# Resident tokens, a reordered program, PSUM banks given out by the list scheduler and a table of priorities in a gated convolution-and-MLP kernel

## The chip, the cores and the metric

The kernel runs on one core of a Trainium2 chip. The time is the device time of one execution in microseconds (us). Every kernel was also timed beside the kernel before on the same chip. The profile is one execution taken by the hardware profiler; its times count from its own first instruction, so a span is some 2 us shorter than the device time. Engines are named as in the profile: PE is TensorE (PEld its weight loads), DVE is VectorE, ACT is ScalarE, POOL is GpSimd, SP is SyncE and SPq its instruction queue, which only issues DMA transfers here.

## The reference

There are 2048 tokens of 640 values. A sigmoid gate, computed from each token, mixes two branches. Branch A is a four-tap convolution of k, times v, then a long convolution over the sequence, times q. Branch B is an MLP of four layers with two layer-norms and shifts by one or two tokens.

```
x  = A_q;  g = sigmoid((x * gate_w).sum(-1))
# branch A
k_shift[t] = sum over j of k[t - j] * shift_k[:, j]        # 4 taps, per channel
kv = k_shift * v
a  = q * (irfft(rfft(pad(kv)) * rfft(pad(ssm_k)))[:2048] + kv * ssm_D)
# branch B
h  = gelu(layernorm(x) @ w1)                               # 640 -> 640
hs = (the four quarters of h shifted by +1, -1, +2, -2 tokens) @ w2
x1 = x + hs
b  = x1 + gelu(layernorm(x1) @ w3) @ w4                    # 640 -> 1536 -> 640
out = g * a + (1 - g) * b
```

The kernels replace the FFT by folded Fourier transforms in blocks, done as matrix products: forward transforms of kv and of the filter, products of the spectra on VectorE (eight "units", one for each of four frequency groups and two channel halves) and inverse transforms.

## The kernel before

Every operation is recorded with the buffers it reads and writes, an engine and an estimated duration. A list scheduler then simulates the five engines and fixes the order of each engine's instructions when the kernel is built; on the chip the engines run these orders strictly in sequence and wait for one another by semaphores.

```
def schedule(self, bw=250.0, tbw=90.0, dlat=1900.0, lat=90.0, backlog=2500.0):
    ...
        for e in ENGS:                                   # pe, act, dve, pool, sp
            ...
            f = free[e]
            for i in cand[e]:                            # whose predecessors are placed
                st = max(f, ready[i])
                ...
                key = (st, -(ops[i].rank + ops[i].bias), i)     # rank: longest way to the end
                if pick is None or key < pick:
                    pick = key
            if best is None or pick < best:
                best = pick
    ...                                                  # the winner is next in its engine's order
```

The biases are all zero in this kernel. The second MLP layer reloads each token tile, adds it in a matrix product, and sends every tile through four engines and a DMA transpose:

```
def mm2(t):
    P.dma(sp, xr[t % 3], A_q[0, 128 * t:128 * (t + 1), :])
    b = mlp_bank()                            # four PSUM banks in a ring for the MLP
    ...
    act(x1[t % 3]..., pr, ACTF.Copy, accum=st[1, 0][:, t:t + 1])
    act(xn2[t % 3], x1[t % 3], ACTF.Square, accum=st[1, 1][:, t:t + 1])
    P.dma(sp, x1s[128 * t:128 * (t + 1), :], x1[t % 3])          # "scratch store"
def ln2(t0, t1):
    ln_math(1, t0, t1)                        # 6 small GpSimd operations
    ... ln_apply: one VectorE operation, then a DMA transpose issued by SyncE
```

The last fifth of the first layer is evicted straight to its four shifted places, 32 partitions at a time:

```
for g in range(4):
    act(hT[32 * g:32 * (g + 1), 4, c0:c0 + 512], ps(b)[32 * g:32 * (g + 1), :], ACTF.Gelu_apprx_tanh)
```

Of the kernel before, what the change touches and what calls it, by code (L numbers as in the profile page):

```python
# [10 lines left out]
BANK = 2048  # L11


class Op:
    __slots__ = ("idx", "eng", "fns", "ins", "outs", "dur", "bias", "nbytes", "preds", "succs", "rank",
                 "tp", "ordinal", "waits", "inc", "value", "dsem", "dval", "snap", "snapd", "start", "end", "order")

    def __init__(self, idx, eng, fns, ins, outs, dur, bias, nbytes):
        self.idx = idx
        self.eng = eng  # L20
        self.fns = fns
        self.ins = ins
        self.outs = outs
        self.dur = dur
        self.bias = bias
        self.nbytes = nbytes
        self.preds = {}
        self.succs = []
        self.inc = False
        self.dsem = None  # L30
        self.tp = False

# [42 lines left out]
def regions(ap):  # L75

    t = ap.tensor
# [3 lines left out]
    if not name.startswith(("arena", "PS")):  # L81
        lo = ap.offset + sum(min(0, s * (n - 1)) for s, n in dims)
        hi = ap.offset + sum(max(0, s * (n - 1)) for s, n in dims) + 1
        return [(name, 0, lo * esz, hi * esz)]
# [12 lines left out]
    psum = name.startswith("PS")  # L97
    out = set()
    for lo, hi in runs:
        b0, b1 = (f0 + lo) * esz, (f0 + hi) * esz  # L100
        if psum:
            b0, b1 = b0 // BANK * BANK, -(-b1 // BANK) * BANK
        for q in range(p0 // 32, (p0 + pcnt - 1) // 32 + 1):
            out.add(("PS" if psum else "SB", q, b0, b1))
# [3 lines left out]
class Prog:  # L108
    def __init__(self, nc):
# [3 lines left out]
        self.bias = 0.0  # L113

    def _record(self, op):
        idx = op.idx
        op.bias += self.bias
# [6 lines left out]
        for ap in op.ins:  # L124
            for reg in regions(ap):
                (ws if reg[0] == "PS" else rs).append(reg)
        for ap in op.outs:
            ws.extend(regions(ap))
        for m, q, lo, hi in rs:
# [17 lines left out]
    def dma(self, queue, out, in_, bias=0.0, transpose=False, slow=False):  # L147
# [9 lines left out]
        issue = 1300.0 if transpose else (700.0 if queue == "pool" else 400.0)  # L157
# [5 lines left out]
    def schedule(self, bw=250.0, tbw=90.0, dlat=1900.0, lat=90.0, backlog=2500.0):  # L163
        ops = self.ops
        for o in ops:
            for p in o.preds:
                ops[p].succs.append(o.idx)
        for o in reversed(ops):
            tail = 0.0
            for s in o.succs:  # L170
                tail = max(tail, ops[s].rank)
            full = o.dur + (o.nbytes / bw + dlat if o.nbytes else lat)
            o.rank = max(tail + full, 0.0)
        left = [len(o.preds) for o in ops]
        ready = [0.0] * len(ops)
        cand = {e: [] for e in ENGS}
        free = {e: 0.0 for e in ENGS}
        dfree = tfree = 0.0
        for o in ops:
            if left[o.idx] == 0:  # L180
                cand[o.eng].append(o.idx)
        order = []
        while True:
            best = None
            for e in ENGS:
                if not cand[e]:
                    continue
                f = free[e]
                pick = None
                for i in cand[e]:  # L190
                    st = max(f, ready[i])
                    if ops[i].nbytes and not ops[i].tp:
                        st = max(st, dfree - backlog)
                    key = (st, -(ops[i].rank + ops[i].bias), i)
                    if pick is None or key < pick:
                        pick = key
                if best is None or pick < best:
                    best = pick
            if best is None:
                break  # L200
            st, _, i = best
            o = ops[i]
            cand[o.eng].remove(i)
            o.start = st
# [4 lines left out]
            elif o.nbytes:  # L209
                t0 = max(st + 0.5 * o.dur, dfree)  # L210
                dfree = t0 + o.nbytes / bw
                o.end = max(dfree, st + o.dur) + dlat
            else:
                o.end = st + o.dur
            o.order = len(order)
            order.append(o)
            for s in o.succs:
                left[s] -= 1
                d = lat
                if ops[s].eng == o.eng and not o.nbytes:  # L220
                    d = 60.0 if ops[s].preds[i] and o.eng != "pe" else 0.0
# [3 lines left out]
        assert len(order) == len(ops)  # L225
# [131 lines left out]
def bass_gated_mix__ssm_conv_h3__mixer_s_mlp__prompt_kernel(  # L357
# [33 lines left out]
    def ps(b, n=1):  # L391
        return PSt[:, 512 * b:512 * (b + n)]

# [5 lines left out]
    oWB = alloc(15360)  # L399
# [6 lines left out]
    oXR = alloc(3 * 640)  # L406
    oX1 = alloc(3 * 640)
    oXN = alloc(3 * 640)
    oX1R = alloc(3 * 640)
# [3 lines left out]
    XF = V(oXF, 20480).rearrange("p (b j r d) -> p b j r d", b=4, j=4, r=2)  # L413
# [8 lines left out]
    w3 = V(oWB, 7680).rearrange("p (c f) -> p c f", c=5)  # L422
    w4 = V(oWB + 7680, 7680).rearrange("p (c f) -> p c f", c=12)
    keo = [V(oWB + 2560 * i, 2560).rearrange("p (e s d) -> p e s d", e=2, s=2) for i in range(2)]
    vin = [V(oWB + 5120 + 1280 * i, 1280).rearrange("p (s d) -> p s d", s=2) for i in range(2)]
    kin = [V(oWB + 7680 + 3200 * i, 3200).rearrange("p (i d) -> p i d", i=5) for i in range(2)]
    kv_hi = V(oWB + 14080, 1280).rearrange("p (s d) -> p s d", s=2)
    kv_lo = V(oPT + 3840, 1280).rearrange("p (s d) -> p s d", s=2)
    kv_rev = V(oX1R, 1280).rearrange("p (s d) -> p s d", s=2)
    kpr = V(oUT, 5120).rearrange("p (s j d) -> p s j d", s=2, j=4)  # L430
    kst = [V(oXF + 2048 * i, 2048).rearrange("p (b n) -> p b n", b=4) for i in range(2)]
    heo_c = [V(oXF + 4096 + 2048 * i, 2048) for i in range(2)]
    heo_t = [V(oXF + 8192 + 2048 * i, 2048) for i in range(2)]
    xT = [V(oXT + 2560 * i, 2560).rearrange("p (c s) -> p c s", c=5) for i in range(3)]
    SHK = V(oYX, 2560).rearrange("p (j d) -> p j d", j=4)
    xin = [V(oPT + 640 * i, 640) for i in range(3)]
    xn1 = [V(oPT + 1920 + 640 * i, 640) for i in range(3)]
# [3 lines left out]
    xr = [V(oXR + 640 * i, 640) for i in range(3)]  # L441
# [36 lines left out]
    def is_ps(ap):  # L478
        return ap.tensor.name.startswith("PS")

    def dve_ns(o, i, mode):
        n = n_of(o)
        if is_ps(o) or any(is_ps(a) for a in i):
# [3 lines left out]
    def tt(o, a, b, op, eng="dve"):  # L487
        P.op(eng, lambda e: e.tensor_tensor(o, a, b, op), [a, b], [o],  # L488
             dve_ns(o, [a, b], 2) if eng == "dve" else 250)

    def ts(o, a, s1, s2, op0, op1=None, eng="dve"):
        aps = [s for s in (s1, s2) if not isinstance(s, (int, float, type(None)))]
        P.op(eng, lambda e: e.tensor_scalar(o, a, s1, s2, op0=op0, **({} if op1 is None else {"op1": op1})),  # L493
             [a] + aps, [o], dve_ns(o, [a], 3) + 60 if eng == "dve" else 250)

    def act(o, a, f, scale=1.0, bias=0.0, accum=None):
        aps = [s for s in (scale, bias) if not isinstance(s, (int, float))]
        P.op("act", lambda e: e.activation(o, a, f, bias=bias, scale=scale, **({"accum_out": accum} if accum is not None else {})),  # L498
# [3 lines left out]
    def mm(o, pairs, split=None):  # L502

        fns = []
        for i, (l, r) in enumerate(pairs):
            fns.append(lambda e, l=l, r=r, i=i: e.matmul(o, l, r, start=(i == 0), stop=(i == len(pairs) - 1)))  # L506
        P.op("pe", fns, [a for p in pairs for a in p], [o], len(pairs) * max(60, n_of(o) / 2.4) + 5)

    sp = "sp"


    P.op("dve", lambda e: e.memset(neghalf, -0.5), [], [neghalf], 70)
# [6 lines left out]
    P.op("dve", lambda e: e.memset(hT[96:128, 4, S:S + 2], 0.0), [], [hT[96:128, 4, S:S + 2]], 70)  # L519
    act(tjunk[:, 1:2], ones[:, 0:1], ACTF.Gelu_apprx_tanh)  # L520
    P.dma("pool", shk_sb.rearrange("p (c j) -> p c j", c=5), A_shift_k.rearrange("(c p) j -> p c j", p=128))
    P.dma("pool", V(oId, 256).bitcast(U16), cI.ap())
    P.dma("pool", Esel.bitcast(U16), cE.ap())
    P.dma("pool", Dcol.rearrange("p (c o) -> p c o", o=1), A_ssm_D.rearrange("(c p o) -> p c o", p=128, o=1), slow=True)
    P.dma("pool", gwT.rearrange("p (c o) -> p c o", o=1), gate_w.rearrange("(c p o) -> p c o", p=128, o=1), slow=True)
    P.dma("pool", V(oR, 2048).bitcast(U16), cR.ap())
    P.dma("pool", w1, B_w1.rearrange("(c p) f -> p c f", p=128))
    for c in range(DC):
        P.dma("pool", w1x[:, c, :].rearrange("p (g f) -> p g f", g=4),
              B_w1[c * 128:(c + 1) * 128, :].rearrange("p (g f) -> p g f", g=4)[:, :, 128:160])  # L530
    for j in range(4):
        P.dma("pool", w2[:, j, :], B_w2[160 * j:160 * j + 128, :])
    for g in range(4):
        P.dma("pool", w2[32 * g:32 * (g + 1), 4, :], B_w2[160 * g + 128:160 * g + 160, :])


    psb = ps(0).bitcast(BF16)
    P.op("pe", [lambda e, c=c: e.transpose(psb[0:4, 128 * c:128 * (c + 1)], shk_sb[:, 4 * c:4 * c + 4], ident)  # L538
                for c in range(DC)], [shk_sb, ident], [psb[0:4, 0:640]], 400)
    act(rows4, psb[0:4, 0:640], ACTF.Copy)  # L540
    for j in range(4):
        pr = ps(2 * (j % 2), 2).rearrange("p (b n) -> p b n", b=2)[:, :, 0:320]
# [3 lines left out]
    mm(ps(0)[:, 0:1], [(ones, gwT[:, c:c + 1]) for c in range(DC)])  # L546
    act(gsum[:, 0:1], ps(0)[:, 0:1], ACTF.Copy)


    cb = [0]  # L550

    def conv_bank(n=1):
        if n == 2:
            b = 4 + 2 * (-(-cb[0] // 2) % 2)
            cb[0] = b - 4 + 2
        else:
            b = 4 + cb[0] % 4
            cb[0] += 1
        return b

    def h_load(c):
        k = kst[c % 2]
        P.dma(sp, k.rearrange("p b n -> p (b n)"), A_ssm_k[128 * c:128 * (c + 1), :])

    def h_chunk(c):
        k, ec, et = kst[c % 2], heo_c[c % 2], heo_t[c % 2]
# [7 lines left out]
        for y in range(4):  # L574
            eo = (0, 1, 1, 0)[y]
            for m in range(2):
                b = conv_bank()
                mm(ps(b), [(Rt[:, y, kk, 128 * m:128 * (m + 1)], ev[:, eo, kk, :]) for kk in range(2)])
                j, r = 2 * (y // 2) + m, y % 2
                src = ps(b).rearrange("p (b c) -> p b c", b=4)  # L580
                lo = 128 * c
                while lo < 128 * (c + 1):
                    hh = lo // 320
# [367 lines left out]
```

## Time and profile before

The median of three runs is 307.29 us (305.7 to 308.86).

| stretch (us) | what runs | limit |
|---|---|---|
| 0 to 91 | layer-norm 1, first layer, filter and k·v work | VectorE |
| 103 to 178.8 | second layer, 16 tiles through four engines and a DMA | latency of the tiles |
| 178.8 to 303.5 | third and fourth layer, inverse transforms | TensorE |

The first part of the page gives each engine's busy time, share and instruction count; the second shows the busy tenths in 40 slices of the span.

```profile
PE 249.3 (81%) x1526; PEld 144.0 (47%) x1526; DVE 229.0 (74%) x352; ACT 151.5 (49%) x289; POOL 87.8 (29%) x156
PE   0401949876797998747899599999999999999994
DVE  4489997989983934948879999999999991121343
```

The table of stretches gives from:to, length, then busy time and instruction count of PE, PEld, DVE, ACT and POOL, the granted clock, the DMA share and GB/s.

```profile
0.00:91.00 91.00, 52.78 (x286) 23.76 (x287) 76.21 (x118) 47.54 (x89) 28.81 (x48) 0.94 0.92 237
103.00:178.80 75.80, 61.60 (x364) 36.30 (x362) 57.54 (x84) 45.87 (x101) 54.41 (x99) 0.93 0.63 172
178.80:303.50 124.70, 124.61 (x816) 79.28 (x816) 87.39 (x142) 48.20 (x83) 1.78 (x5) 1.00 0.21 56
```

The chain of waits (start, length, what) ends in one piece of TensorE work. Below it stands the line for the scratch stores from the view of one tile: durations, then the first and last start.

```profile
171.47 5.74 DMA arena<-arena
178.80 124.63 PE PSall L506 x816
L156 SPq DMA_DIRECT2D x_scratch<-arena x16: 319/452/581, 107.5 to 175.7; - x16
```

So TensorE has nothing but work from 178.8 us on, and the question for any change is how much sooner that state can begin. The 16 tiles of the second layer stand alone from 107.5 to 175.7 us, at 4.5 us a tile.

### The profile page before, as it was taken

Reading aid. Unit: us, or ns where it says so; the run is one execution under the profiler, and the core shown is the slowest. Engines: PE = TensorE matmul, PEld = TensorE weight load, DVE = VectorE, ACT = ScalarE, POOL = GpSimd, SP = SyncE. Lnnn points to the kernel's source line nnn. Section 1 sums busy time; section 2 is a strip of 40 time slices with the busy share of each in tenths; the row PEclk is TensorE's granted clock in tenths of the full one; section 3 lists DMA queues with packets and bytes.
Section 4 is the critical chain, followed back from the end, with each engine's and each line's share of the span. In section 5 each row is a group of like instructions: output and inputs, shape, how many; then the busy total and the mean of one; then the engine's idle time right before and its main releaser. Section 6 shows DMA issues by size and latency. Waiting matters only on the chain.

```text
span 307.5 us, 4162 instructions
## 1 busy us (share of the span) xinstructions
PE 249.3 (81%) x1526; PEld 144.0 (47%) x1526; DVE 229.0 (74%) x352; ACT 151.5 (49%) x289; POOL 87.8 (29%) x156
## 2 busy tenths in 40 slices
PE   0401949876797998747899599999999999999994
PEld 0101314432353575424456357456645664777773
DVE  4489997989983934948879999999999991121343
ACT  1400577975588799732844321622462155333342
POOL 6265602021032256866968840000000000000000
PEclk9999997996999999887999799999999999999999
DMA  7978999978934047996633630004101311023342
GB/s 238 308 244 155 340 170 270 384 216 227 196 79 115 6 124 212 250 331 161 184 78 93 182 106 21 23 0 107 45 0 35 96 43 45 24 83 87 107 132 84
DMA packets 54708, 43.04 MB, mean 140 GB/s; under 512 B 34204, under 2 KB 50592, under 8 KB 54560
## 3 DMA queue, kind: packets, MB, share of 16 engines
q1 hardware_dynamic: 52848, 35.40, 44.8%
q0 software_dynamic: 1840, 7.39, 7.8%
q8 instruction: 12, 0.20, 0.3%
q14 instruction: 8, 0.07, 0.1%
HBM read 29.66 MB, written 5.24 MB: 114 GB/s over the span
## 4 chain that ended last, share of the span: by engine, by line
PE 52%; DVE 21%; DMA 11%; POOL 8%; ACT 4%; issue 3%; SPq 0%; ACTq 0%; POOLq 0%
PE PSall L506 51%; DVE arena L488 16%; DMA arena<-arena 8%; ACT arena L498 4%; POOL arena L652 3%; DVE arena L645 2%; POOL arena L488 2%; DMA arena<-in_A_shift_k_dram 2%; POOL arena L493 2%; DMA arena<-in_A_ssm_k_dram 2%; DVE arena L493 1%; POOL arena L661 1%; POOL arena L156 1%; DVE arena L646 1%; SPq L153 0%
## 5 line engine op out<-in xcount | busy, mean ns | idle before, releaser
L506 PE MATMUL PSall<-arena 128*128 128x320 bf16 (+3 forms) x1521 | 248.6, 323 | 46.2 <-ACT arena L498 14.2
L488 DVE TENSOR_TENSOR arena<-arena 128x640 bf16<-128x640 bf16 (+8 forms) x253 | 199.1, 836 | 51.0 <-ACT arena L498 43.4
L506 PEld LDWEIGHTS PSall<-arena 128*128 128x128 bf16 (+1 forms) x1521 | 143.5, 100 | 151.1 <-issue 32.5
L498 ACT ACTIVATE arena<-PSall 128x512 bf16<-128x512 f32 (+4 forms) x190 | 109.0, 613 | 85.6 <-PE PSall L506 68.5
L498 ACT ACTIVATE arena<-PSall,arena 128x320 bf16<-128x320 f32 (+1 forms) x48 | 29.5, 616 | 56.0 <-PE PSall L506 52.9
L493 POOL TENSOR_SCALAR arena<-arena 128x1 f32<-128x1 f32 (+2 forms) x44 | 23.0, 524 | 74.9 <-DVE arena L646 55.7
L493 DVE TENSOR_SCALAR arena<-arena 128x640 bf16<-128x640 bf16 (+2 forms) x36 | 15.5, 450 | 20.6 <-POOL arena L488 20.3
L488 POOL TENSOR_TENSOR arena<-arena 128x1 f32<-128x1 f32 (+2 forms) x60 | 24.4, 411 | 12.6 <-DVE arena L493 8.9
L498 ACT ACTIVATE arena<-arena 128x640 bf16<-128x640 bf16 (+2 forms) x18 | 12.2, 679 | 10.2 <-DMA arena<-arena 10.0
L645 DVE BATCH_NORM_STATS2 arena<-arena 128x6 f32<-128x320 bf16 x32 | 13.8, 473 | 3.0 <-DMA arena<-in_A_q_dram 3.0
L661 POOL TENSOR_TENSOR arena<-arena 128x1 f32<-128x1 f32 x16 | 12.9, 804 | 1.1
L156 POOL DMA_DIRECT2D arena<-in_B_w_dram x16 | 11.2, 703 | 2.6 <-PE PSall L506 2.6
L652 POOL TENSOR_TENSOR arena<-arena 128x2 f32<-128x2 f32 (+1 forms) x9 | 11.7, 1301 | 0.7
L538 PE MATMUL PSall<-arena 128*4 128x128 bf16 x5 | 0.7, 302 | 8.0 <-DMA arena<-in_A_shift_k_dram 8.0
L538 PEld LDWEIGHTS PSall<-arena 128*4 128x4 bf16 x5 | 0.4, 109 | 8.0 <-DMA arena<-in_A_shift_k_dram 8.0
L498 ACT ACTIVATION_READ_ACCUMULATOR arena<-PSall 128x1 f32 x16 | 3.2, 201 | 0.0
L646 DVE BATCH_NORM_AGGREGATE arena<-arena 128x2 f32<-128x12 f32 x16 | 3.1, 200 | 0.1
L498 ACT ACTIVATION_READ_ACCUMULATOR arena<-arena 128x1 f32 x16 | 3.1, 195 | 0.0
L498 ACT ACT_TABLE_LOAD x1 | 1.3, 1283 | 0.7 <-PEq L936 0.7
L770 DVE MEMSET arena<- 1x640 uint32 x2 | 1.2, 592 | 0.3 <-DVE arena L493 0.2
L156 POOL DMA_DIRECT2D arena<-in_A_ssm_D_dram x1 | 1.0, 999 | 0.0
L156 POOL DMA_DIRECT2D arena<-cI x1 | 0.8, 754 | 0.8 <-POOLq L936 0.8
(19 smaller groups left out, 6.1 us busy)
## 6 DMA issues: line engine op xcount, KB each, us to landing
arena<-in_A_q_dram SPq DMA_DIRECT2D x48, 160.0 KB, 3.3
arena<-in_A_k_dram SPq DMA_DIRECT2D x7, 800.0 KB, 5.7
arena<-in_B_w_dram POOLq DMA_DIRECT2D x2, 1920.0 KB, 10.1
arena<-in_A_ssm_k_dram SPq DMA_DIRECT2D x5, 512.0 KB, 5.0
arena<-in_A_v_dram SPq DMA_DIRECT2D x8, 320.0 KB, 4.4
x_scratch<-arena SPq DMA_DIRECT2D x16, 160.0 KB, 2.9
arena<-x_scratch SPq DMA_DIRECT2D x16, 160.0 KB, 2.3
out_dram<-arena SPq DMA_DIRECT2D x16, 160.0 KB, 2.3
```

Of the source, the lines that this page charges most:

```text
L156: fn = lambda e: e.dma_start(out, in_, **kw)
L488: P.op(eng, lambda e: e.tensor_tensor(o, a, b, op), [a, b], [o], dve_ns(o, [a, b], 2) if eng == "dve" else 250)
L493: P.op(eng, lambda e: e.tensor_scalar(o, a, s1, s2, op0=op0, **({} if op1 is None else {"op1": op1})), [a] + aps, [o], dve_ns(o, [a], 3) + ...
L498: P.op("act", lambda e: e.activation(o, a, f, bias=bias, scale=scale, **({"accum_out": accum} if accum is not None else {})), [a] + aps, [ ...
L506: fns.append(lambda e, l=l, r=r, i=i: e.matmul(o, l, r, start=(i == 0), stop=(i == len(pairs) - 1)))
L538: P.op("pe", [lambda e, c=c: e.transpose(psb[0:4, 128 * c:128 * (c + 1)], shk_sb[:, 4 * c:4 * c + 4], ident) for c in range(DC)], [shk_sb, ...
L645: P.op("dve", lambda e, o=o, i=i: e.bn_stats(o, i), [i], [o], 420)
L646: P.op("dve", lambda e: e.bn_aggr(bna[:, t, :], bns[k]), [bns[k]], [bna[:, t, :]], 130)
L652: P.op("pool", lambda g: g.tensor_tensor(r, e, neghalf[:, t0:t1], ALU.pow), [e, neghalf[:, t0:t1]], [r], 600)
L661: P.op("pool", lambda e: e.tensor_tensor(s[5], s[3], neghalf[:, t0:t1], ALU.pow), [s[3], neghalf[:, t0:t1]], [s[5]], 600)
L770: P.op("dve", lambda e: e.memset(H[0:1, 1], 0.0), [], [H[0:1, 1]], 400)
```

## The change

Its intent is to run the second layer's slow tile chain beside the k·v work and to take load off the early stage. It has six parts: the tokens stay in SBUF for the second layer; layer-norm 1 and the first layer come first in the program; the k·v work is split into two channel halves; PSUM banks are no longer fixed rings but given out by the scheduler; some transposes go from DMA to TensorE; and each group of operations gets a bias from a table of 389 numbers. The diff, cut to its core:

```diff
+    BIASES = {'combine-0-1|dve': 1782800.0,
+     'combine-0-2|dve': 287000.0,
...                                                 (389 entries, ns, from -2.7e6 to 2.9e6)
+    P.biases.update(BIASES)
     def schedule(self, quota, ...):                # PSUM: a bank is chosen when a tile's first
+                    if live[t.cls] >= quota[t.cls] or t.turn != turn[t.cls]:
+                        continue                   # operation is placed
-    def kv_half(b, hi, dst):
+    def kv_half(g, b, hi, dst):                    # 320 channels of k and v: runs of 640 bytes
+    keo, vin, kin, kv_hi in oW4                    # k·v staging shares w4's space
-        P.dma(sp, xr[t % 3], A_q[0, 128 * t:128 * (t + 1), :])
-            pairs.append((ident, xr[t % 3][:, hs]))
+            pairs.append((ident, xs[t // 4][:, t % 4, hs]))     # tokens are resident
-                for g in range(4):
-                    act(hT[32 * g:32 * (g + 1), 4, c0:c0 + 512], ps(b)[32 * g:..., :], Gelu)
+                act(hx[sc % 2], pr, ACTF.Gelu_apprx_tanh)       # one Gelu of 128 partitions
+                for g in range(4):                              # and four SBUF copies
+                    P.dma(sp, hT[32 * g:32 * (g + 1), 4, c0:c0 + 512], hx[sc % 2][32 * g:..., :])
+            if t >= PET:                                        # PET = 4: the first four tiles
+                ln_apply(...)                                   # are transposed on TensorE
+    for sc in range(4):                             # new program order
+        x_load(sc); ln1(...); mm1(sc)
+    gate; h_load and h_chunk; mm2 and ln2 of 12 tiles; w3_load; mm3(0); the other 4 tiles;
+    then kv_block, x_fwd and combine of both halves; w4_load; mm4(0..3); ...
```

The new layer-norm 2 also needs four GpSimd operations instead of six. The diff changes more than the six parts: the scheduler's own costs are new (a plain issue on SyncE costs 0.47 us instead of 0.40, a 128x640 transpose 1.46 instead of 1.30, a small GpSimd operation 0.45 instead of 0.25), loads of constants and of w1 go from GpSimd's queue to ScalarE's or SyncE's, and the q loads of the output stage go from SyncE's queue to GpSimd's.

## The prediction

> **What bounds the kernel now.** Three stages.
>
> - 0 to 91 us: VectorE. The stretches table gives it 7 to 10 us busy of every 10 from 10 us on: layer-norm 1, filter folding and the k·v preparation are interleaved. TensorE gets work only as VectorE delivers it.
> - 103 to 178 us: a latency chain. The 16 tiles of the second MLP layer pass through TensorE, ScalarE, GpSimd, VectorE and a DMA transpose, with three buffers. Their scratch stores (queue timeline) are issued from 107.5 to 175.7 us, 4.5 us a tile; VectorE is 5 to 10 us busy of 10 (it waits 43.4 us for ScalarE in all).
> - 178.8 to 303.5 us: TensorE. The chain of waits is one piece of 124.6 us with 816 matmuls; the stretches show 10.0 of 10 busy.
>
> TensorE is busy 249.3 us of 307.5. At the pace of the stretch 280 to 290 us (76 matmuls of 320 columns, 0.132 us each) its 1008 x 320 and 420 x 512 columns are, estimated, 222 us of work, 97 us of it before 178.8 us: about 80 us are lost there.
>
> **What the change does.**
>
> - Order: layer-norm 1 and the first MLP layer come first, so the 4.5 us-per-tile chain runs beside the k·v work, not after it. This is the main gain.
> - PSUM: eight shared banks placed by the scheduler, not two fixed rings (TensorE waited 14.2 us for ScalarE).
> - Tokens resident: 16 reloads of 160 KB and their 3.3 us landings go. Four DMA transposes (4.4 us to landing) become 20 TensorE transposes with ScalarE evictions.
> - ScalarE: sixteen 32-partition Gelus (589 ns) become four full ones (601 ns) plus 16 small DMAs, 7 us less. GpSimd: 4 instead of 6 operations per layer-norm-2 tile (414 to 804 ns each).
> - VectorE, estimated from measured shapes: k·v halves 8 x 5.94 = 47.5 us become 16 x 3.27 = 52.4; with folding and combining +7 us, on 229.
> - k and v are read in 640-byte runs. The Trainium skill ("DMA: Bandwidth & Descriptors", Specifications) wants 512 B for line rate, so I expect little loss; the trace cannot confirm it.
>
> **How much is critical.** A new gate: w4 takes the space of the k·v staging, so it loads (10.1 us) only after the last k·v block. VectorE's work until then is layer-norm 1 24 + filter 13 + k·v 60 + layer-norm-2 applies 7 = 104 us; with start-up and idle 115. w4 is there near 125 us. TensorE then still has mm4 55, mm3 of three chunks 38, inverse transforms 34 = 127 us, plus some 6 left over and a 4 us end: 262 us. VectorE's path (115 + combine 10 + eight units 103 + last inverse 17 + 4) ends near 249, so TensorE still finishes last.
>
> **Prediction: 262 us, range 249 to 281.** Faster by over 2%: 0.95; within 2%: 0.035; slower: 0.015.
>
> **What would show it.** Scratch stores start before 60 us and end near 115. The last k·v multiplication is near 110 us. The saturated TensorE piece that ends the chain starts near 130. TensorE busy falls by up to 15 us, VectorE rises to about 235, ScalarE falls to about 143.
>
> **What would make it wrong.** The hand-fed priorities fit a model, not the chip: in-order queues may stall behind one late transfer. The DMA traffic of the first 180 us (about 36 MB) must pass in some 125; if transposes and 640-byte runs limit it, everything shifts by 10 to 20 us. If VectorE ends last, the units set the end.

## The result, and the profile after

The changed kernel takes 284.4 us in the median (283.07 to 284.78, four runs) where the kernel before takes 308.08 beside it. The ratio is 0.925 (0.918 to 0.932). All ratios here are the mean time of one kernel's fast runs over that of the other's fast runs of the same rounds, so they are not quite the ratio of the medians. A control of the same kernel among the later runs gave 283.95 us and 0.922. The prediction of 262 us, and its range up to 281, were too optimistic.

The same lines of the page after the change:

```profile
PE 242.9 (86%) x1531; PEld 146.5 (52%) x1546; DVE 232.5 (82%) x399; ACT 142.5 (50%) x257; POOL 76.6 (27%) x124
PE   0078879939999959969999999979999999999994
DVE  3769797759889389866799999999999999999242
```

The busy times are nearly those predicted (VectorE "about 235", ScalarE "about 143"). What moved is the idle time. The stretches below end where three things happen: 135.9 us is the end of the last k·v work on VectorE, 148.7 the first product with w4, 277.8 the end of the last inverse transform.

```profile
0.00:33.00 33.00, 14.44 (x85) 7.56 (x87) 21.60 (x67) 10.01 (x17) 12.97 (x27) 1.00 0.97 251
33.00:100.00 67.00, 59.24 (x375) 33.26 (x379) 51.73 (x84) 49.26 (x88) 23.44 (x40) 0.95 0.88 201
100.00:135.90 35.90, 29.27 (x179) 17.54 (x178) 30.06 (x48) 25.77 (x56) 26.35 (x39) 0.95 0.98 218
135.90:148.70 12.80, 12.65 (x64) 6.38 (x66) 11.38 (x17) 7.33 (x13) 2.34 (x4) 1.00 0.80 257
148.70:277.80 129.10, 126.92 (x833) 81.71 (x837) 116.78 (x184) 49.64 (x85) 11.48 (x15) 1.00 0.22 55
```

Read the third busy number, VectorE. Until 135.9 us it is busy 21.60 + 51.73 + 30.06 = 103.4 us, where 104 was predicted, and idle 32.5 us, where 11 was allowed: 11.4 us of it up to 33 us, 15.3 up to 100, 5.8 up to 135.9. That the busy time fits is partly luck: when the trace's instructions are matched to the program, 7.4 of the 103.4 us are combines and the first products of a unit, which the prediction had put behind this point, and the work that it did count takes 96.0. After 148.7 us next to nothing is lost: 129.1 us for what was predicted as 127, with TensorE busy 126.92.

Here are five pieces of the chain of waits, then the scratch stores, then lines of the table of waits (who waits for whom: us in all, times, longest), then two lines of GpSimd's timeline and one of TensorE's (start, length, what; in brackets the idle time before it and what ended it).

```profile
51.51 5.19 SPq L204
57.37 5.78 DMA arena<-in_A_v_dram
95.06 4.92 DMA arena<-in_A_k_dram
145.87 4.81 DMA arena<-arena
227.22 50.97 PE PSall L996 x348
L207 SPq DMA_DIRECT2D x_scratch<-arena x16: 319/573/837, 43.3 to 134.7; - x16
POOL arena L207 <- DVE arena L978: 110.6, 13, 40.5
DVE arena L978 <- DMA arena<-in_A_k_dram: 7.6, 3, 5.8
DVE arena L978 <- DMA arena<-in_A_v_dram: 6.0, 2, 3.4
DVE arena L1143 <- DMA arena<-in_A_q_dram: 5.3, 3, 2.6
DVE arena L983 <- POOL arena L1147: 4.3, 5, 1.3
139.66 1.13 POOL L207 DMA_DIRECT2D arena<-in_B_w_dram  x1 [2.46 <-PE PSall L996]
194.20 0.80 POOL L207 DMA_DIRECT2D arena<-in_A_q_dram  x1 [40.50 <-DVE arena L978]
135.94 16.26 PE L996 MATMUL PSall<-arena 128*128 128x320 bf16 x87 [0.51 <-DVE arena L978]
```

The scratch stores start at 43.3 us as hoped, but end at 134.7 instead of 115. The gate that the prediction named exists: GpSimd's queue issues the w4 load at 139.66 us, when TensorE's last forward transform of k·v data frees the space, it lands at 148.6, and the first product with w4 starts at 148.7. (The longest wait of that queue, 40.5 us, is not this load but one of q for the output stage.) But no engine waits at the gate itself: TensorE waits 0.51 us for the last k·v work, starts at 135.94 us and then works through the gate, 12.65 of the 12.8 us before it on other work. Its last idle time of note ends with the k·v work. (Whether products with w4, loaded sooner, could have filled TensorE's earlier idle time was not tried.) VectorE waits for k and v loads 13.6 us, for tokens 5.3 us, for GpSimd 4.3 us. Between 33 and 100 us, 13% of the chain of waits are SyncE's issues and 20% the landings of transfers; the durations of SyncE's 66 issues there, added up from its timeline, are 62.5 us of 67. Among them are the 16 SBUF copies that the change moved from ScalarE, 11.7 us.

### The profile page after: what moved, and what is told of

Read it like the earlier page. It is cut to its first block, busy times and chain, and to the rows that moved or that the text cites. A ratio compares the mean times of both kernels' runs of the same rounds, so it can differ in the third digit from the quotient of the medians.

```text
span 282.4 us, 4190 instructions
## 1 busy us (share of the span) xinstructions
PE 242.9 (86%) x1531; PEld 146.5 (52%) x1546; DVE 232.5 (82%) x399; ACT 142.5 (50%) x257; POOL 76.6 (27%) x124
## 4 chain that ended last, share of the span: by engine, by line
PE 48%; DVE 21%; DMA 12%; POOL 6%; ACT 4%; SPq 4%; issue 2%; ACTq 0%; DVEq 0%; POOLq 0%
PE PSall L996 48%; DVE arena L978 20%; ACT arena L988 4%; POOL arena L983 4%; DMA arena<-in_A_shift_k_dram 4%; DMA arena<-arena 3%; SPq L204 2%; DMA arena<-in_B_w_dram 2%; DMA arena<-in_A_v_dram 2%; SPq L207 2%; DMA arena<-in_A_k_dram 2%; POOL arena L1147 1%; DVE arena L983 1%; POOL arena L207 0%; PE PSall L1199 0%
## 5 line engine op out<-in xcount | busy, mean ns | idle before, releaser
L996 PE MATMUL PSall<-arena 128*128 128x320 bf16 (+3 forms) x1506 | 240.0, 319 | 20.6 <-DVE arena L978 13.7
L978 DVE TENSOR_TENSOR arena<-arena 128x640 bf16<-128x640 bf16 (+7 forms) x299 | 203.9, 731 | 28.6 <-ACT arena L988 12.7
L988 ACT ACTIVATE arena<-PSall 128x512 bf16<-128x512 f32 (+4 forms) x158 | 100.8, 686 | 63.3 <-PE PSall L996 42.7
L983 POOL TENSOR_SCALAR arena<-arena 128x1 f32<-128x1 f32 (+2 forms) x60 | 34.5, 577 | 68.3 <-ACT arena L988 41.4
L207 POOL DMA_DIRECT2D arena<-in_A_q_dram x16 | 11.9, 744 | 110.6 <-DVE arena L978 110.6
L1147 POOL TENSOR_TENSOR arena<-arena 128x1 f32<-128x1 f32 (+1 forms) x25 | 19.7, 790 | 1.3
L207 POOL DMA_DIRECT2D arena<-in_B_w_dram x14 | 8.9, 637 | 13.0 <-PE PSall L996 13.0
L1199 PE MATMUL PSall<-arena 128*128 128x128 bf16 x20 | 2.3, 312 | 0.0
L978 POOL TENSOR_TENSOR arena<-arena 128x16 f32<-128x16 f32 x3 | 1.3, 435 | 3.0 <-DVE arena L983 2.9
L1199 PEld LDWEIGHTS PSall<-arena 128*128 128x128 bf16 x20 | 2.1, 146 | 0.0
## 6 DMA issues: line engine op xcount, KB each, us to landing
arena<-in_A_q_dram SPq DMA_DIRECT2D x3, 640.0 KB, 13.1
```

The source lines that it names most:

```text
L207: fn = lambda e: e.dma_start(out, in_, **kw)
L978: P.op(eng, lambda e: e.tensor_tensor(o, a, b, op), [a, b], [o], dve_ns(o, [a, b], 2) if eng == "dve" else 450)
L983: P.op(eng, lambda e: e.tensor_scalar(o, real(a), s1, s2, op0=op0, **({} if op1 is None else {"op1": op1})), [a] + aps, [o], dve_ns(o, [a] ...
L988: P.op("act", lambda e: e.activation(o, real(a), f, bias=bias, scale=scale, **({"accum_out": accum} if accum is not None else {})), [a] + ...
L996: fns.append(lambda e, l=l, r=r, i=i: e.matmul(real(o), l, r, start=(i == 0), stop=(i == len(pairs) - 1)))
L1147: P.op("pool", lambda g: g.tensor_tensor(o, a, e, ALU.pow), [a, e], [o], 300 + 400 * n_of(o))
```

## The experiments

Two theories were at hand for the 22 us between the prediction and the result.

- **A, the queue.** SyncE issues loads, stores and transposes strictly in sequence and is full from 33 to 100 us. The change put 16 copies on it to spare ScalarE 7 us that ScalarE did not lack.
- **B, the order.** The engine orders fit the scheduler's costs, which are not the chip's. Waits that the scheduler thought hidden come due on the chip, first here, then there.

A rival to both is that the rearrangement itself brings less than thought, whatever the order.

### The queue: copies moved, and doubled

In the first, only the issuing engine of the copies changes after scheduling; every other instruction keeps its place. In the second, a 2-KB transfer between two DRAM buffers is issued behind each copy.

```diff
+    for o in sched:                                   # e1_hx_act
+        if o.nbytes and o.grp.startswith("mm1-") and o.grp.endswith("|sp"):
+            o.eng = "act"
+        more.append(o)                                # e2_sp_extra
+        if o.nbytes and o.grp.startswith("mm1-") and o.grp.endswith("|sp"):
+            ... e.dma_start(junk[n], A_v[0, 16 * n:16 * (n + 1), 0:64]) ...
+            more.append(d)
```

> Order of every engine frozen as in the changed kernel (284.4 us); only the 16 small SBUF copies of the last first-layer chunk (0.73 us of SyncE's issue each, 11.7 us in all, all between 33 and 100 us) are issued from ScalarE instead. Theory A (SyncE's in-order issue of transfers bounds the stretch 33 to 100 us): that stretch shrinks by 8 to 11 us, total 274 to 278 us. Rival B (the DMA engines' throughput bounds it): the traffic is the same, total 283 to 286. Rival C (VectorE or GpSimd latency bounds it): 283 to 286, or slower if ScalarE is held up.

> Frozen order; behind each of those 16 copies SyncE issues one extra 2 KB transfer (DRAM to DRAM) that nobody waits for: some 0.5 us more issue each, 32 KB more traffic in all. Theory A: 7 to 10 us slower, 291 to 295. Rivals B and C: 284 to 286.

Without the copies on SyncE: 281.53 us (281.32 to 281.71), ratio 0.908 (0.902 to 0.913). With the extra issues: 290.92 us (290.69 to 292.88), ratio 0.940 (0.932 to 0.948). The stretch 33 to 100 us of the first, then of the second:

```profile
33.00:100.00 67.00, 59.37 (x380) 33.25 (x383) 55.58 (x90) 50.68 (x90) 25.42 (x41) 0.97 0.97 219
```

```profile
33.00:100.00 67.00, 56.68 (x350) 31.27 (x354) 50.48 (x81) 45.89 (x82) 19.75 (x39) 0.92 0.81 185
```

VectorE does 3.9 us more work in the stretch (55.58 against 51.73), or 1.3 us less. The last inverse transform ends at 275.4 and 284.4 us instead of 277.8. So the queue is a real limit for this order, and both directions show it. But 10 us of queue time (62.5 to 52.4) are worth only 2.4 us in the profiled runs, 2.9 in the medians and some 5 by the ratios: VectorE's idle time in the stretch falls by no more than 3.9 us. The first run lies between what Theory A and its rivals expected (274 to 278, 283 to 286), the second at the edge of what Theory A expected. Theory A holds and is small.

### Longer runs and an earlier start

The next two test the two other suspects in the early stage: k and v read in 640-byte pieces, and the taps' load, which lands 10.95 us after its issue at the head of the chain. The first reads contiguous runs of 3200 and 1280 bytes and so puts wrong values in place on purpose (the comparison with the reference still passed, so it would not catch such an error). The second issues the taps and the small w1 slices first on their queues.

```diff
-            P.dma(sp, kt, bass.AP(A_k.tensor, k0 + (t0 - 3) * D, [[2 * D, 128], [D, 5], [1, 320]]))
+            P.dma(sp, kt.rearrange("p i d -> p (i d)"), bass.AP(A_k.tensor, k0 + (t0 - 3) * D, [[2 * D, 128], [1, 1600]]))
-        P.dma(sp, vt, A_v[0, t0:t0 + 256, ds].rearrange("(p s) d -> p s d", s=2))
+        P.dma(sp, vt.rearrange("p s d -> p (s d)"), bass.AP(A_v.tensor, A_v.offset + t0 * D, [[2 * D, 128], [1, 640]]))
```

```diff
+    first = [o for o in sched if o.grp in ("const-shk|sp", "const-w1x|act")]      # e4_taps_first
+    sched = first + [o for o in sched if o not in first]
```

> Wrong result on purpose. Frozen order; the k and v loads keep their bytes and buffers but read one contiguous run per partition (3200 and 1280 bytes) instead of 640-byte runs (five and two). Rival B (640-byte runs and DMA throughput bound the early stage): 6 us or more faster, 272 to 278. Theory A: 283 to 285, unless SyncE's issue of such a transfer itself gets shorter than 0.6 us.

> Frozen order except that the 5 KB load of the filter taps is SyncE's first transfer (before: seventh; its first user ran at 14.6 us) and the five loads of the 32-column weight slices are ScalarE's first. Theory A with a late start: taps are there by 7 us, SyncE no longer idles from 7.5 to 18.5 us behind them, everything moves forward: 275 to 280. If the start has slack (SyncE's total issue time alone counts from 18 us on): 283 to 285.

Long runs: 281.64 us (280.05 to 283.49), ratio 0.908 (0.901 to 0.915). Taps first: 282.41 us (281.94 to 284.7), ratio 0.912 (0.905 to 0.919). The last inverse transform ends 4.1 and 2.1 us earlier in the profiled runs. The prediction had named the Trainium skill ("DMA: Bandwidth & Descriptors", Specifications) for 512 bytes as the least transfer at line rate and expected "little loss" from 640-byte runs; the runs agree that it is little, 1 to 1.5% of the time, but not nothing. That it is the rate of the transfers is not shown. The k loads after 33 us land 4.3 us after their issue in the mean in both kernels (six known landings each), and VectorE's wait for them stays at 7.6 us; the v loads land after 3.6 us instead of 4.0, and their issue takes SyncE 0.48 us instead of 0.60. So the gain may as well be queue time. Each suspect again gives 2 to 4 us, less than its expectation had (272 to 278 and 275 to 280).

### The copies undone, and both together

Here the copies go altogether: as in the kernel before, four Gelus of 32 partitions write straight to the places. The order is otherwise frozen. The second adds the early taps.

```diff
-                act(hx[sc % 2], pr, ACTF.Gelu_apprx_tanh)           # e5_hx_direct, in effect
-                for g in range(4): P.dma(sp, hT[32 * g:..., 4, c0:c0 + 512], hx[sc % 2][32 * g:..., :])
+                for g in range(4): act(hT[32 * g:..., 4, c0:c0 + 512], pr[32 * g:..., :], Gelu)
```

> One part undone, order frozen: the last first-layer chunk is again evicted as four 32-partition Gelus straight to their shifted places, the 16 SBUF copies are gone. SyncE loses 11.7 us of issue between 33 and 100 us and the copies' 2.9 us landings, ScalarE gains 7 us. Theory A (SyncE's issue bounds that stretch) plus the landings: 277 to 281, at least as good as the copies issued from ScalarE (281.5). If the change's trade was right: 284 to 288.

> The previous one with the taps' load first on SyncE and the weight slices first on ScalarE. If both costs lie on the same chain one after the other, their gains add: 274 to 279. If the second only fills a wait that the first leaves: 277 to 281.

Direct Gelus: 279.62 us (276.89 to 280.17), ratio 0.906 (0.898 to 0.913). With early taps too: 279.26 us (277.19 to 280.31), ratio 0.905 (0.898 to 0.913). This part of the change, which was meant as a saving, costs about 4 us in the order it was given. And the gains do not add: the early start that was worth some 2 us alone is worth 0.4 here. About 17 us are still missing.

### The change without its table

> Control: the changed kernel again, on the chip of the next three. 284 us, ratio to the kernel before 0.925.

> All of the change, but the table of hand-fed priorities is empty, as it was in the kernel before. If my prediction's reading is right (the order of the program itself, first layer first, brings the gain), it stays clearly faster than before: 280 to 295 us. If the gain lives in the priorities, it is as slow as before or slower: 305 to 340 (the scheduler's own estimate of its end, part of the kernel, goes from 255 to 318 us; that of the changed kernel is 27 us below what the chip took).

```diff
-    P.biases.update(BIASES)
```

The control ran at 283.95 us (282.84 to 285.85). Without the table the same operations take 338.18 us (337.88 to 338.74), ratio 1.098 (1.090 to 1.106): slower than the kernel before by a tenth. Its stretches from 90 us on, the last piece of its chain, and its scratch stores:

```profile
90.00:141.00 51.00, 44.19 (x258) 22.68 (x259) 29.24 (x54) 31.22 (x55) 13.52 (x22) 0.89 0.41 90
141.00:204.50 63.50, 32.22 (x154) 15.95 (x152) 63.00 (x99) 19.15 (x44) 46.58 (x47) 0.75 0.40 110
202.70 129.25 PE PSall L995 x837
L207 SPq DMA_DIRECT2D x_scratch<-arena x16: 324/432/608, 70.4 to 210.1; - x16
```

The program puts the second layer before the k·v work, but that only numbers the operations. The scheduler ranks by the longest way to the end, and puts VectorE's spectrum products before the layer-norm-2 applies: from 141 to 204.5 us VectorE is busy 63.00 of 63.5 us, nearly all of it with those products (the last k·v work is done at 131.2 us, earlier than in after), while TensorE gets 32.22 us of work, at a mean granted clock of 0.75. The last stretch of TensorE is the same 129 us as in the tuned kernel, but starts 54 us later. So the program's rearrangement does not gain by itself. The gain of 24 us needs the table, and the table is worth 54 us. What a table searched for the program of the kernel before would bring was not tried, so how much of the gain needs the rearrangement stays open. An experiment with PSUM in fixed rings under the new program could not be made: the scheduler finds no way on with the new limits on open tiles. What the shared banks are worth alone stays open; the trace shows only that TensorE waits 2.9 us for ScalarE instead of 14.2.

### New costs, new table

That makes Theory B the question. By the scheduler's own simulation the changed kernel ends at 255.2 us; the chip's span is 282.4. Matching the trace's instructions to the program's operations in sequence gives the chip's costs:

| cost | scheduler (us) | trace of after (us) |
|---|---|---|
| plain issue on SyncE | 0.47 | 0.63 |
| issue of a 128x640 transpose on SyncE | 1.46 | 1.30 |
| start of TensorE's last matmul (320 columns) to ScalarE's start | 0.23 (0.14 of it the matmul) | 0.34 |
| eviction of 640 columns with row sum on ScalarE | 0.85 | 0.72 |
| taps' load, issue to landing | about 4.5 | 10.95 |
| one 640-KB token load at the start, issue to landing | 6.8 | 13.1 |
| GpSimd's small layer-norm-2 operation | 0.45 | 0.42 in the median, 0.59 in the mean, up to 2.2 |

Replaying the fixed order of after with such costs ended at 277 us. One of the measured costs seems too high, by an estimate of 0.13 us for each hand-over: the new scheduler adds 0.335 us to the simulated end of TensorE's work, but the trace's 0.34 us count from the start of the last matmul. (From its modelled end to ScalarE's start the trace shows 0.04.) The next three kernels use this. The first has the changed kernel's operations, the measured costs and a table searched anew (simulated annealing over the biases, on the simulated end with the nominal and with randomly lengthened costs). The second also has the direct Gelus. The third is the control: the same search for as long with the scheduler's own costs.

```diff
+    def recost(self):                                  # s1, s2: costs as measured
+        ...
+            if o.tp:
+                o.dur, o.dl = 311.0 + o.nbytes / 165.8, 2200.0
+            elif o.nbytes:
+                o.dur = 475.0 if g.startswith("x_load") else {"sp": 635.0, "pool": 600.0, "act": 470.0}[o.eng]
+    LAT = {"pe-act": 335.0, "pe-dve": 270.0, "pe-sp": 330.0, ...
-    BIASES = {...}
+    BIASES = {...}                                     # s1, s2 and s3: another table
```

> The changed kernel's program, operation for operation, with nothing altered but the numbers that the list scheduler orders it by: the costs are those measured in the trace of after (a plain SyncE issue 0.635 us instead of 0.47, a 128x640 transpose issue 1.30 instead of 1.46, a GpSimd operation 0.46 to 1.20 as seen, landing times per kind of transfer as seen, a hand-over from TensorE to ScalarE 0.335 instead of 0.09), and the table of priorities is searched anew against them, for the nominal costs and for randomly lengthened ones together. Replayed with these costs, the order of after ends at 277 us (its span on the chip was 282.4), the new order at 261. Theory B (most of the missed 22 us is engine orders fitted to wrong costs): 264 to 273 us, last product of keys and values done by 116 to 124 instead of 136, first product with w4 at 130 to 138 instead of 148.7. Theory A (the missed time sits in SyncE's in-order queue and in the work itself, which this kernel leaves as it is): 278 to 284.

> As the kernel with measured costs, and the 16 SBUF copies of the last first-layer chunk replaced by four Gelus of 32 partitions each, part of the program that the search orders (not patched in afterwards). The replay ends at 259. If the copies' queue time adds to the wrong costs: 261 to 270 us and 2 to 4 us below the kernel with measured costs. If a good order hides the copies already: within 2 us of it. This is meant as the version that beats both kernels.

> Control for the search: the changed kernel with its own costs, and its table searched on by the same method for as long. By its own costs the end moves from 255.2 only to 253.9 us, so the table was at its optimum there. Theory B: no more than the luck of another order, 277 to 284 us (a replay with the measured costs gives 273 where after's gives 277). If longer search alone were what helps, it would come near the kernel with measured costs, 264 to 273.

| kernel | median (us) | range | ratio to before |
|---|---|---|---|
| measured costs | 280.53 (two fast runs: 277.14, 278.47) | 277.14 to 283.39 | 0.897 (0.890 to 0.904) |
| measured costs, direct Gelus | 273.38 | 271.67 to 276.15 | 0.880 (0.873 to 0.887) |
| own costs, searched on | 279.12 | 278.36 to 279.49 | 0.901 (0.896 to 0.905) |

The first two had two and one slow runs of four. The first misses what Theory B expected and is hardly better than the control, which itself gained some 5 us although by its own costs it improved by only 1.3: another order alone can be worth that much, by luck. The trace of the first, which is of a slow run (282.6 us), shows where it lost time. Early in its chain stands this, and its TensorE waits so:

```profile
8.66 10.43 DMA arena<-cI
PE PSall L1079 <- DMA arena<-cI: 19.1, 1, 19.1
```

The identity matrix, needed for the first TensorE transposes, is issued ninth on its queue and lands at 19.1 us. The new costs gave each early load the fixed landing that it had in the trace of after, where the identity was issued first; in the kernel's own simulation it lands at 14.2 us. On the chip the early loads land as the bytes issued before them are moved; about 300 bytes per ns plus 2.3 us fits the early landings of these kernels to about 1.5 us in the mean, an estimate from their traces. The kernel had lost some 5 us against its simulation by 35 us.

This is not the whole of it. The second kernel has the same first costs, its identity lands at 6.65 us, and it takes 273.4 us. That is above the 261 to 270 expected, but 5 us below the first kernel in the fast runs, where 2 to 4 were given to the copies, and only 1 us above the same program in the next round. So part of the first kernel's loss is the luck of its order.

The second error was GpSimd. Between 100 and 125 us its small operations often take far longer than their median. Here is one group of them in after, with VectorE beside it:

```profile
116.77 3.13 POOL L983 TENSOR_SCALAR arena<-arena 128x1 f32<-128x1 f32 x3
117.08 2.01 DVE L978 TENSOR_TENSOR arena<-arena 128x640 bf16<-128x640 bf16 x2
```

One of the three, an operation on one value per partition, starts at 117.72 us and takes 2.19 us; VectorE starts a product with two inputs in SBUF at 117.59 (1.49 us), and another two-input operation at 119.00. The Trainium skill ("SBUF — State Buffer", Who interferes with whom) states that a VectorE instruction with two SBUF inputs contends with a GpSimd instruction that reads SBUF, and that the loser is blocked, not slowed. This trace agrees: seven of the first eight GpSimd operations of over 1.2 us start 0.05 to 0.25 us after a VectorE operation with two inputs of over 1.1 us, and the eighth 0.85 us after one; of the 79 shorter GpSimd operations only two start within 0.3 us after one. (The skill's page "Perfetto Trace Analysis", GPSIMD Engine Instruction, advises start-to-start spacing over reported durations; where an operation was alone, at 109.53 us, the two agree: 1.66 us reported, the next instruction 1.61 us later.)

### Second costs

Both errors were mended: landings wait for earlier bytes, and GpSimd's operations cost their mean. The search now weighs six sets of randomly lengthened costs more than the nominal ones. Besides the same operations (s5) there are the direct Gelus (s4), and the direct Gelus with eight tiles transposed on TensorE instead of four (s6).

```diff
-                o.dl = next(v for k, v in self.PLAIN if g.startswith(k)) ...
+                o.dl = next((v for k, v in self.LAND if g.startswith(k)), 2300.0)
-                    o.dur = {700.0: 640.0, 1100.0: 1200.0}.get(o.dur, 636.0 if g.startswith("gate") else 455.0)
+                    o.dur = {700.0: 760.0, 1100.0: 900.0}.get(o.dur, 730.0 if g.startswith("gate") else 330.0 if g.startswith("ln1") else 600.0)
-    BIASES = {...}
+    BIASES = {...}
-    PET = 4                                            # s6 only
+    PET = 8
```

> The changed kernel's program again, only the scheduler's costs and table differ. The kernel with measured costs lost 6 us in its first 35 us (the model had early loads land late for a fixed reason, while on the chip they land as the bytes issued before them are moved, about 300 bytes per ns, plus 2.3 us; the search had put the identity matrix last) and 5 us more between 112 and 125 us (GpSimd's small operations took 0.6 us in the mean and up to 1.7, the model said 0.455). Both are corrected, and the search weighs six sets of randomly lengthened costs more than the nominal ones. Replay: 257.0 nominal, 273.7 in the mean of twenty unseen sets. Theory B (orders fitted to wrong costs are most of the missed 22 us): 266 to 275 us, keys and values done by 123 to 130, first product with w4 at 135 to 143. If costs cannot be known well enough for such orders (each search finds the model's remaining errors): 277 to 283, like the kernel with measured costs.

> The same second costs for the program with direct Gelus in place of the 16 copies. Replay: 256.1 nominal, 270.6 in the mean of the unseen sets. Theory B: 263 to 271 us, below the first kernel with direct Gelus and measured costs (273.4). Against the kernel with second costs alone it shows what the copies are worth in an order made for either: 0 to 4 us.

> As the kernel with second costs and direct Gelus, and the first eight token tiles transposed on TensorE instead of four, which takes 4 more transposes of 1.3 us each off SyncE's queue before 60 us. Replay: 254.1 nominal, 269.9 in the mean of the unseen sets. 262 to 270 us, within 3 us of the one with four.

| kernel | median (us) | range | ratio to before |
|---|---|---|---|
| second costs, the change's operations | 272.49 | 271.76 to 273.89 | 0.880 (0.876 to 0.885) |
| second costs, direct Gelus | 272.32 | 271.84 to 272.67 | 0.879 (0.875 to 0.883) |
| second costs, direct Gelus, eight tiles | 272.74 (two fast runs: 269.48, 270.41) | 269.48 to 275.29 | 0.871 (0.866 to 0.877) |

The first row is the test: operation for operation the changed kernel, and 11.5 us faster than the control of it (ratios of 0.880 and 0.922 to the kernel before, each on its own chip). Its stretches, with the same three events at their ends (last k·v work 123.3, first product with w4 137.7, last inverse transform 266.7):

```profile
0.00:33.00 33.00, 16.29 (x94) 8.60 (x96) 23.52 (x65) 11.36 (x19) 15.27 (x27) 1.00 1.02 256
33.00:100.00 67.00, 62.07 (x396) 33.90 (x400) 62.73 (x103) 53.11 (x94) 31.01 (x42) 0.97 1.04 229
100.00:123.30 23.30, 21.53 (x144) 13.52 (x144) 18.26 (x30) 18.22 (x42) 19.39 (x30) 1.00 1.03 242
123.30:137.70 14.40, 14.20 (x71) 6.82 (x70) 11.76 (x19) 9.53 (x19) 10.87 (x11) 1.00 0.74 236
137.70:266.70 129.00, 126.78 (x831) 81.66 (x837) 117.74 (x184) 49.64 (x85) 11.14 (x15) 1.00 0.22 55
DVE arena L1013 <- DMA arena<-in_A_k_dram: 2.0, 2, 1.7
137.81 1.40 PE L1031 MATMUL PSall<-arena 128*128 128x320 bf16 x9 [0.26 <-DMA arena<-in_B_w_dram]
```

From 33 to 100 us VectorE does 62.73 us of work instead of 51.73; its idle time there falls from 15.3 to 4.3 us, and its wait for k loads from 7.6 to 2.0. That is the gain: the last k·v work is done 12.6 us earlier, and what follows moves with it, the first product with w4 from 148.7 to 137.7 us; TensorE waits for w4 only 0.26 us. SyncE's issues from 33 to 100 us still add up to 62.3 us, as in after (62.5). So the full queue was no limit as such, but only in the order of after; the orders of all five engines changed together, and no run takes SyncE's alone.

A second measure does not depend on the total. Each kernel carries its scheduler, which can be run again and set beside the trace. The last k·v work ends later on the chip than in the kernel's own simulation by 23.8, 22.8 and 17.8 us in the three kernels ordered on the old costs (after, own costs searched on, and the one of the next section), and by 11.1 to 14.9 us in the five ordered on measured costs. That is what Theory B says. But the first measured costs (13.6 and 11.1 us) do no worse there than the second (11.4, 14.9 and 13.4), and the kernel of the first row is still 6.5 us behind its simulation at 35 us. That mending the two errors brought the gain over the first round is not shown.

The second row agrees: with an order made for it, the program without the copies is no faster than the one with them (272.32 and 272.49), though undoing the copies in the frozen order gave 4 us. Its time lies just outside what was expected (263 to 271). Eight tiles on TensorE give the best fast runs (269.48 and 270.41), but two of its four runs were slow. Any of the three beats both kernels; the quick one to recommend is the second row, whose four runs were all fast.

### Which of the two, costs or slack

> Takes the kernel with second costs apart. It differs from the changed kernel by two things together: costs measured in a trace, and a search against randomly lengthened costs beside the nominal ones. Here the costs are the changed kernel's own and only the search is against lengthened ones; its own end is 255.3 (255.2 before), the mean of twenty unseen lengthened sets falls from 275.0 to 267.6. If slack against delays is what brings the gain: 270 to 275 us, like the kernel with second costs (272.5). If the costs bring it: 277 to 284, like the control that searched on with its own costs (279.1). A replay of its order with the second costs gives 265.4, where that of the changed kernel's order gives 268.4.

```diff
-    BIASES = {...}
+    BIASES = {...}      # own costs; searched against lengthened ones as in the kernels above
```

281.43 us (280.83 to 281.95), ratio 0.911 (0.905 to 0.917). A table searched for slack, but on the old costs, gains 2.5 us on the control; the other 9 us of the 11.5 were not reached without measured costs. This rests on one table for each side, and orders differ by some 5 us by luck; but all three on the old costs (284.0, 279.1 and 281.4 us) are slower than all three on the second costs (272.3 to 272.7 in the medians).

## Why the prediction was wrong

- **The structure was right.** The w4 load waits for the last k·v data (issued at 139.7 us, landed at 148.6). Behind it TensorE works almost without a gap: 129.1 us, predicted as 127 for the products with w4, those of three chunks with w3 and the inverse transforms. TensorE finished last. But no engine waits at the gate itself; TensorE works almost without a gap from the end of the k·v work at 135.9 us. Scratch stores started before 60 us (43.3).
- **Costed work was right in the sums, partly by luck.** VectorE's work until the k·v work is done was predicted as 104 us and is 103.4. But the kinds of work in that sum take 96.0 us; 7.4 us of combines and first products had been put later. VectorE in all 232.5 (about 235), ScalarE 142.5 (about 143), TensorE down 6.4 us (up to 15).
- **The step that failed is "VectorE's work until then … 104 us; with start-up and idle 115."** It gave 11 us to idling; the trace has 32.5. The start-up alone (to 33 us) takes 11.4. The stretches behind it, with 15.3 and 5.8 us idle, had been given nothing. The last k·v work therefore ends at 135.9 us instead of 115. From there to the first product with w4 it is 12.8 us where 10 were allowed, because the load is issued only at 139.7 us, after the last forward transform, as the last reader of the staging buffers; TensorE fills them with 12.65 us of other work, where 6 were thought to be left over. Behind the gate 1.3 us were won back: 135.7 us to the end of the device time, predicted as 137. The sum is 20.9 + 2.8 - 1.3 = 22.4 us, the whole miss.
- **"This is the main gain", said of the order of the program, was wrong.** Without the table the reordered program is 9.8% slower than the kernel before. The gain needs the 389 priorities; whether they would have gained as much in the old program was not tried. The prediction named them only as a risk: "The hand-fed priorities fit a model, not the chip: in-order queues may stall behind one late transfer." That risk is in the main what happened, and it should have been in the sum: the kernel before, simulated by its own scheduler, ends at 285.2 us and runs a span of 307.5 on the chip. That 22 us are also the size of the miss is chance: the changed kernel is 27 us behind its simulation, and the prediction did not start from one.
- **About half of the miss is the order; why the rest was missed stays in part open.** With the same operations and an order made on measured costs, idle time before the end of the k·v work falls from 32.5 to 18.8 us, and the time to 272.5 us. Of the remaining 10 us to the prediction, 7.8 are idle time (18.8 against 11) and 4.4 lie between the last k·v work and the gate (14.4 against 10), less what is won elsewhere. Half of that idle time, 9.5 us, lies before 33 us, where the DMA share is 1.02, so the transfers there probably cannot come much faster. Whether a better order could take more of the rest stays open.
- **"16 small DMAs, 7 us less" for ScalarE was a saving in the wrong place.** In the given order it costs 4 us; in the orders made on the second costs nothing.
- **"Little loss" from 640-byte runs** was about right: some 3 us of 284 in the medians, and it is not shown that the rate of the transfers was the cause.
- **"If VectorE ends last"** came close: in the kernel with second costs 42% of the chain are VectorE's two-input operations, in after 20%.

## What to carry to other kernels

A predicted gain that rests on overlap should carry an idle time taken from the trace of the old kernel, in every stretch and not only at the start: here the busy time of VectorE came out as predicted and the miss was idle time. Orders fixed in advance are only as good as the costs they were searched with. Take these from the chip's trace, look in the new trace for costs that are still wrong (here the landing of one load and one kind of small operation), and make several orders before judging, since two orders made on the same costs can lie some 5 us apart. And do not judge a part of such a program in a frozen order: what costs 4 us there may cost nothing once the order is made for it.

## What the Trainium skill lacked or had wrong

- "DMA: Bandwidth & Descriptors", Issuing engines are not separate DMA queues: it says that issuing from several engines only saves the sequencer's time to initiate, "usually small relative to the DMA itself". Here 66 issues took SyncE 62.5 of 67 us, 0.59 us in the median for a plain transfer, 1.3 for a 128x640 transpose and 2.4 to 5.2 for a filter transpose. Moving 16 issues to ScalarE won 2.9 us in the medians, and 16 more cost 6.5. The section has no such durations. How far the queue limits depends on the order: in another it was as full (62.3 us) and the kernel 11.5 us faster.
- "DMA: Bandwidth & Descriptors", Specifications: 512 bytes is given as the least transfer for line rate. The runs do not contradict it (k loads in runs of 640 and of 3200 bytes land after the same 4.3 us), but no page that I found says what the length of the runs does to the issue: v loads took SyncE 0.60 us in runs of 640 bytes and 0.48 in runs of 1280.
- "DMA: Bandwidth & Descriptors", Anatomy of one DMA: its fit of about 2.0 us plus bytes at 436 bytes per ns is given per DMA, on GpSimd's path. At the start of these kernels, with a dozen transfers open, landings of 2 to 15 us fit 2.3 us plus all bytes issued before at about 300 bytes per ns. No section that I found says how to cost a transfer in a crowd.
- "SBUF — State Buffer", Who interferes with whom: the rule fits, but the section does not say what it does to small operations: GpSimd's layer-norm operations on one value per partition (without the power) took 0.42 us in the median, 0.59 in the mean and up to 2.2.
- No page that I found gives the time from the end of one engine's work to the start of the work on another that waits for it: in these traces about 0.03 us from VectorE to SyncE's queue or ScalarE, 0.06 from ScalarE to TensorE, 0.04 from TensorE's modelled end to ScalarE.
